# Sigmoid attention with a top-1 mixture of experts: attention in groups of two units, a joint gate for the first two batches, output stores without an order

## The chip, the cores and the metric

The kernel runs on one core of a Trainium2 chip. A core has five engines that run their own instruction queues: TensorE (PE, matrix products), VectorE (DVE), ScalarE (ACT), GpSimd (POOL) and SyncE (SP, which here only issues DMAs). They wait for one another through semaphores. The metric is the time of one launch in device microseconds, the median of three runs.

## The reference

For q, k and v of 8 batches, 12 heads, 448 tokens and 64 features in float32, attention with a sigmoid, and on its output a mixture of 8 experts that gives each token to one expert:

```python
scores = scale * np.matmul(q, k.transpose(0, 1, 3, 2)) - np.log(S)
attn = np.matmul(1 / (1 + np.exp(-scores)), v)            # 8 x 12 x 448 x 64
x = attn.transpose(0, 2, 1, 3).reshape(3584, 768)
logits = x @ w_gate                                       # 768 x 8
expert_idx = argmax(logits); gate_w = softmax(logits) at expert_idx
for e in range(8):                                        # w1: 768 x 1024, w2: 1024 x 768
    out[mask] = gate_w[mask, None] * (relu(x[mask] @ w1[e]) @ w2[e])
```

## The kernel before

**Attention** is cut into 24 units of two head pairs (a batch has three units, and `g` numbers the head pairs), and a unit into `ST` = 7 steps. `scores` (L608) makes one step's score tiles on PE, a product of 64x64 pieces into two tiles of the pool `sc` (4 buffers), and `squash` (L600) puts two sigmoids on ACT that turn them into `at` (8 buffers). `weighted` (L620) multiplies `at` by the values `vn` into two tiles `av` that gather over the 7 steps. After the seventh, `tokens` (L488) transposes the two tiles on DVE into `xt`, which SP stores to `x_tok` in DRAM once three head pairs have gathered, and `copy_tokens` (L644) copies the same tiles to `xf` on ACT, for the gate. Scores run two steps ahead of the weighted sums, so a unit starts with two steps squashed.

**The experts.** `moe` (L224) computes one slot of 448 tokens with one expert's weights, seven slots in all (`NS`). The first layer (L240) is 8 tiles of 18 matmuls of 128x128 by 448 columns, each three products of high and low parts; ACT's Relu (L247) and a DVE operation (L248) empty a tile. The second layer (L263) is 6 tiles of 24 matmuls; DVE multiplies a tile by the gate (L276) and transposes it (L277). A slot is 288 matmuls, in two alternating tiles of the pool `moe`. Weights come through SP into `wst` and are split by ACT (L159) and POOL (L160) into parts ahead of their use. `store` (L214) puts a quarter of an output tile on SP.

**The order** is written by hand: `attention` (L673) is a generator over steps `s`, 178 in all, and from step `START` = 70 on it yields twice a step, and each time 7 expert matmuls (`MIX`) are put on the queues. Steps 0 to 69 hold ten units of attention alone. From then on each unit is one burst: at its fifth step (`BURST` = 4) all its 7 steps go to PE in a row (L784 to L789), then experts again. So there are 14 bursts, and a burst can stand in the middle of an expert tile. In the burst of some units `split_tokens` (L472) prepares the next slot's tokens on DVE and ACT.

**Keys, queries and values.** `READY` (L665) loads (`load_pair`, `load_values`, 4 buffers each) and transposes (`turn`, L565, DVE) the next unit's operands at the first four steps of each unit.

**The gate** of a batch: `gate_a` (L286) makes logits of the batch's `xf` (PE, `psg`, 12 products of 32 columns), `gate_b` transposes them (PE, `pl`) and finds the best expert by small DVE operations, `gate_c` counts tokens per expert with a product by `ones` (PE, `pc`) and picks the batch's expert, `gate_d` ranks the tokens with two more products (PE, `pr`), and `gate_d2` scatters records from POOL. `PLACES` tells at which step each stage goes: those of batches 0 and 1 in the part with attention alone, at even steps, each between two pieces of attention.

## Time and profile before

| | us |
|---|---|
| median of 3 runs | 776.85 (776.73 to 777.79) |
| the profiled execution's own time | 776.84 |
| its span, first to last instruction | 775.0 |
| outside the span | 1.84 |
| attention alone, 8.6 to 125.8 | 117.2 |
| experts with 14 bursts of attention, 125.8 to 557.6 | 431.8 |
| experts alone and the end, 557.6 to 769.5 | 211.9 |

PE counts as busy 99% of the span. Its matmuls overlap in the records, since each one's end lies beyond the start of the next, so a PE that is always busy may still lose time between two kinds of work. What a matmul costs is therefore read from the distance between the starts of two rows, not from a row's length. ACT is busy 50%, DVE 48% and POOL 45% of the span.

### The profile page before, as it was taken

How to read it: one execution, taken by the hardware profiler on the slowest of the kernel's cores; microseconds unless marked ns; L12 is line 12 of the kernel's file. 1: busy time of each engine (PE TensorE's matmuls, PEld its weight loads, DVE VectorE, ACT ScalarE, POOL GpSimd, SP SyncE). 2: the span in 40 equal slices, each digit the busy share in tenths (PEclk: the TensorE clock that was granted, in tenths of full speed). 3: DMA queues.
4: the chain of work that ended last, by engine and by line, in shares of the span. 5: the costliest groups of instructions: out<-in, count | busy, mean ns of one | idle time of the engine just before them, and what ended most of it. 6: DMA issues, size and time to landing. Idle time of an engine off the chain costs nothing. (4 is left out here: it accounts for less than half of the span.)

```text
span 775.0 us, 15532 instructions
## 1 busy us (share of the span) xinstructions
PE 768.4 (99%) x5586; PEld 593.3 (77%) x5586; DVE 373.9 (48%) x806; ACT 384.1 (50%) x688; POOL 349.6 (45%) x330
## 2 busy tenths in 40 slices
PE   9999999999999999999999999999999999999997
PEld 6555557687696786867868769677698999999996
DVE  2354584465264652537426384254736493244543
ACT  5877776645536455264443653545523342444451
POOL 8648554242352342531615316054265764664351
PEclk9999999999999999999999999999999999999999
DMA  9777798976758846587585876766167554655770
GB/s 207 169 160 157 171 251 197 210 171 154 169 129 173 201 107 166 139 190 168 116 194 84 193 169 144 183 168 166 38 171 170 157 146 118 202 143 155 220 223 38
DMA packets 311633, 125.67 MB, mean 162 GB/s; under 512 B 210062, under 2 KB 307006, under 8 KB 311552
## 3 DMA queue, kind: packets, MB, share of 16 engines
q1 hardware_dynamic: 305504, 112.42, 61.9%
q0 software_dynamic: 5760, 11.76, 5.4%
q8 instruction: 45, 0.74, 0.4%
q10 hardware_dynamic: 288, 0.46, 0.2%
q14 instruction: 36, 0.29, 0.1%
HBM read 102.49 MB, written 22.49 MB: 161 GB/s over the span
## 5 line engine op out<-in xcount | busy, mean ns | idle before, releaser
L602 ACT ACTIVATE at<-sc,bias_s 128x448 f32<-128x448 f32 x336 | 192.3, 633 | 107.4 <-PE sc L616 106.5
L160 POOL TENSOR_TENSOR w1l<-wst,w1h 128x768 fp32r<-128x768 f32 x72 | 132.7, 1853 | 173.9 <-ACT w1h L159 172.2
L160 POOL TENSOR_TENSOR w2l<-wst,w2h 128x512 fp32r<-128x512 f32 x84 | 107.0, 1298 | 138.7 <-ACT w2h L159 121.0
L616 PE MATMUL sc<-qt,kt 64*64 64x448 f32 x1344 | 167.3, 545 | 0.0
L632 PE MATMUL av<-at,vn 64*64 64x448 f32 x1344 | 165.0, 536 | 0.0
L240 PE MATMUL ps<-xh,w1h 128*128 128x448 f32 x336 | 124.4, 370 | 0.2 <-DVE nw L439 0.2
L240 PE MATMUL ps<-xh,w1l 128*128 128x448 f32 x336 | 123.4, 367 | 0.0
L240 PE MATMUL ps<-xl,w1h 128*128 128x448 f32 x336 | 123.3, 367 | 0.0
L263 PE MATMUL ps<-hh,w2l 128*128 128x448 f32 x336 | 123.3, 367 | 0.0
L263 PE MATMUL ps<-hl,w2h 128*128 128x448 f32 x336 | 123.2, 367 | 0.0
L263 PE MATMUL ps<-hh,w2h 128*128 128x448 f32 x336 | 122.7, 365 | 0.0
L616 PEld LDWEIGHTS sc<-qt,kt 64*64 64x64 f32 x1344 | 78.2, 189 | 56.9 <-issue 44.4
L632 PEld LDWEIGHTS av<-at,vn 64*64 64x64 f32 x1344 | 59.4, 133 | 64.3 <-issue 53.5
L159 ACT CAST w2h<-wst 128x512 fp32r<-128x512 f32 x108 | 64.7, 620 | 75.7 <-PE ps L263 64.5
L247 ACT ACTIVATE hh<-ps 128x448 fp32r<-128x448 f32 x56 | 30.6, 546 | 139.6 <-PE ps L240 137.0
L276 DVE TENSOR_TENSOR ps<-ps,gt 128x448 f32<-128x448 f32 x42 | 40.7, 969 | 85.4 <-PE ps L263 85.3
L495 DVE STREAM_TRANSPOSE xt<-av 128x448 f32<-128x448 f32 x46 | 27.3, 629 | 101.5 <-PE av L632 100.4
L248 DVE SCALAR_TENSOR_TENSOR hl<-ps,hh 128x448 fp32r<-128x448 f32 x56 | 34.4, 614 | 78.3 <-ACT hh L247 76.8
L240 PEld LDWEIGHTS ps<-xh,w1h 128*128 128x128 f32 x336 | 63.1, 188 | 9.9 <-issue 4.4
L263 PEld LDWEIGHTS ps<-hh,w2l 128*128 128x128 f32 x336 | 65.2, 194 | 6.6 <-issue 3.5
L263 PEld LDWEIGHTS ps<-hl,w2h 128*128 128x128 f32 x336 | 65.2, 194 | 6.2 <-issue 3.2
L263 PEld LDWEIGHTS ps<-hh,w2h 128*128 128x128 f32 x336 | 65.2, 194 | 3.4 <-DVE nw L439 0.2
(158 smaller groups left out, 918.9 us busy)
## 6 DMA issues: line engine op xcount, KB each, us to landing
wst<-in_moe_w_dram SPq DMA_DIRECT2D x72, 384.0 KB, 3.3
wst<-in_moe_w_dram SPq DMA_DIRECT2D x54, 512.0 KB, 5.1
x_tok<-xt SPq DMA_DIRECT2D x64, 168.0 KB, 2.8
qn<-in_q_dram SPq DMA_DIRECT2D x184, 56.0 KB, 3.1
raw<-x_tok SPq DMA_DIRECT2D x28, 336.0 KB, 6.2
out_dram<-ob SPq DMA_DIRECT2D x84, 112.0 KB, 2.4
kn<-in_k_dram SPq DMA_DIRECT2D x104, 56.0 KB, 3.3
kn<-in_k_dram POOLq DMA_DIRECT2D x80, 56.0 KB, 4.0
```

The source lines that it names most:

```text
L159: nc.scalar.copy(hi, st)
L160: eng.tensor_tensor(lo, st, hi.bitcast(F32), op=ALU.subtract)
L240: nc.tensor.matmul(ps[:, :S], a[:, ws], b_, start=(t == 0 and n == 0), stop=(t == KD - 1 and n == 2))
L247: nc.scalar.activation(hh[:, :S], ps[:, :S], AF.Relu)
L248: nc.vector.scalar_tensor_tensor(hl[:, :S], ps[:, :S], 0.0, hh[:, :S].bitcast(F32), op0=ALU.max, op1=ALU.subtract)
L263: nc.tensor.matmul(ps[:, :S], a, b_, start=(j == 0 and n == 0), stop=(j == KF - 1 and n == 2))
L276: nc.vector.tensor_tensor(by_gate, by_gate, gate_rows[b], op=ALU.mult)
L495: nc.vector.transpose(xts[b][:, :, t, :], pv[:, :S].rearrange("p (j s) -> p j s", s=32))
L602: nc.scalar.activation(at, ps[:, :S], AF.Sigmoid, bias=bias_s, scale=SCALE)
L616: nc.tensor.matmul(ps[quarter(g, h), :S], ks, ops[g, "q"][OWN[h]], start=True, stop=True)
L632: nc.tensor.matmul(psv[g][OWN[h], :S], ops[g, "v"][rows, c, :], at[rows], start=(c == 0), stop=(c == KC - 1))
```

## The change

**Groups of two.** From step 70 on only even units have a burst, and it holds 14 steps, this unit's and the next one's: 7 groups. Within it the first two scores stand together, turns (transposes) for the unit after the next follow at steps 5, 7, 8 and 9 (`TURNS`), the first unit's tiles are emptied in the middle, and its `av` tiles are taken from the experts' pool. `to_boundary` puts the rest of the current expert tile ahead of the group, and `mixed` takes these matmuls off later yields. `gate_a` of batches 4 and 6 goes to the end of a group. The tokens of slots 1 and 3 are split in a later group (`IN_NEXT`), those of slot 5 in `moe`.

**Loads.** Pairs are loaded two units ahead and three (`FIRST_OF_TWO`), values for both units of a group while the odd unit's steps pass (`SECOND_OF_TWO`); the values of unit 11 come from POOL's queue.

**Joint gates.** Batches 0 and 1 are gated together by `early_b` to `early_d`, on tiles of both (DVE operations twice as wide), at the steps of batch 1. The ranks come from the products by `ones` and `upper` in `early_c`, so neither has a `pr`. Their eight record scatters move from steps 34 to 62 to steps 70 to 86.

**Stores.** All output stores are declared apart from one another, and `keep_tokens` puts the `x_tok` stores one yield later.

```diff
 def store():
+            nc.sync.nop()
-            apart(put, stored.setdefault((d, i), []))
+            apart(put, stored)
...
+    def early_b():
+        for b, lo in enumerate((logits_0, logits)):
+            for c in range(2):
+                at = (2 * b + c) * P
+                nc.tensor.transpose(pl[:GP, at : at + P], lo[:, c * GP : (c + 1) * GP], ident)
...
+    def early_c(oh, z):
+        for n, of in enumerate((ones, upper)):
+            nc.tensor.matmul(
+                pc[:, n * n2 : (n + 1) * n2], of[:GP], oh.rearrange("p c e -> p (c e)"), start=True, stop=True
+            )
+        nc.vector.tensor_copy(sums, pc[:, : 2 * n2])
...
+    def early_d(b, lm, sums, cnt):
+        nc.vector.tensor_copy(pre[:, 0], base)
+        for c in range(1, NCH):
+            nc.vector.tensor_add(pre[:, c], pre[:, c - 1], sums[:, 0, c - 1])
...
-                if u % 2 == 0 and s < START - ST:
+                if u % 2 == 0 and (s < START - ST or s >= START):
                     psv[g] = ps_moe.tile([P, 512], F32, tag="moe", name=f"av_{g}")
...
+    FIRST_OF_TWO = {5: lambda u: load_pair(2 * u + 6), 6: lambda u: load_pair(2 * u + 7)}
+    SECOND_OF_TWO = {i: lambda u, i=i: load_values(2 * u + 2 + i) for i in range(4)}
+    TURNS = {5: (0, "k"), 7: (0, "q"), 8: (1, "k"), 9: (1, "q")}
...
-        EARLY = {5: "b", 7: ("c", "c2"), 9: ("l", "c3"), 11: "d", 13: "g", 32: "e"}
+        EARLY = {5: "B", 7: "C", 9: ("l", "C3"), 11: "D", 13: "g", 32: "e"}
-            places = (EARLY, EARLY, FIRST_LATE, LATE, LATE, LATE, LATE, LAST)[b]
+            places = ({}, EARLY, FIRST_LATE, LATE, LATE, LATE, LATE, LAST)[b]
...
+        def to_boundary():
+            at = (NS * PER_SLOT - left) % PER_SLOT
+            one = 3 * KD if at < PER_SLOT // 2 else 3 * KF
+            return -(at - (0 if at < PER_SLOT // 2 else PER_SLOT // 2)) % one
...
-            yield s, MIX[0]
+            yield s, mixed(MIX[0])
+            keep_tokens()
             if s >= START:
+                if i == BURST and u % 2 == 0 and s < N_ST:
+                    n = to_boundary()
+                    ahead[0] += n
+                    yield s, n
...
-                if i == BURST:
-                    for n in range(ST):
-                        score_to(a + n + 3)
+                if i == BURST and u % 2 == 0:
+                    for n in range(2 * ST):
+                        score_to(a + max(n, 1) + 3)
                         weigh_to(a + n + 1)
-                        if n == ST - 1:
+                        if n == 2 * ST - 1 and u % 3 == 2:
+                            gate_a(u // 3)
+                        if n % ST == ST - 1:
                             copy_tokens()
...
+                        if n in TURNS:
+                            g, nm = TURNS[n]
+                            turn(2 * u + 4 + g, nm)
```

The next two pieces are PE's order where unit 14 (head pairs 28 and 29) ends; `sc` are scores, `av` weighted sums, `ps2` a second-layer tile. Before:

```order
L616 MATMUL sc_30_1_3705<-qt_30_3495,kt_30_3452 64x448 x2
L616 MATMUL sc_31_1_3706<-qt_31_3564,kt_31_3534 64x448 x2
L632 MATMUL av_28_3593<-at_28_6_3670,vn_28_3119 64x448 x2
L632 MATMUL av_29_3596<-at_29_6_3672,vn_29_3207 64x448 x2
L263 MATMUL ps2_1_0_0_3554<-hh_1_6_3500,w2l_1_11_3505 128x448
L263 MATMUL ps2_1_0_1_3732<-hh_1_0_3077,w2h_1_8_3413 128x448
```

The same place in the change:

```order
L742 MATMUL sc_30_1_3676<-qt_30_3466,kt_30_3423 64x448 x2
L742 MATMUL sc_31_1_3677<-qt_31_3533,kt_31_3503 64x448 x2
L758 MATMUL av_28_3572<-at_28_6_3639,vn_28_3162 64x448 x2
L758 MATMUL av_29_3575<-at_29_6_3641,vn_29_3209 64x448 x2
L742 MATMUL sc_30_2_3696<-qt_30_3466,kt_30_3423 64x448 x2
L742 MATMUL sc_31_2_3697<-qt_31_3533,kt_31_3503 64x448 x2
L758 MATMUL av_30_3706<-at_30_0_3659,vn_30_3240 64x448 x2
L758 MATMUL av_31_3709<-at_31_0_3661,vn_31_3288 64x448 x2
```

Unit 15 (head pairs 30 and 31) now follows without expert matmuls between, and the second-layer tile has been finished ahead of the group.

ACT's order at the same place; `at` are sigmoids, `xf` the copies for the gate, `w2h` weight parts. Before:

```order
L602 ACTIVATE at_30_1_3711<-sc_30_1_3705,bias_s_82 128x448
L602 ACTIVATE at_31_1_3713<-sc_31_1_3706,bias_s_82 128x448
L654 COPY xf_28_3725<-av_28_3593 128x448
L654 COPY xf_29_3727<-av_29_3596 128x448
L159 CAST w2h_1_13_3739<-wst_1_10_3182 128x512
L159 CAST w2h_1_14_3751<-wst_1_11_3376 128x512
```

In the change:

```order
L728 ACTIVATE at_30_1_3682<-sc_30_1_3676,bias_s_82 128x448
L728 ACTIVATE at_31_1_3684<-sc_31_1_3677,bias_s_82 128x448
L780 COPY xf_28_3692<-av_28_3572 128x448
L780 COPY xf_29_3694<-av_29_3575 128x448
L728 ACTIVATE at_30_2_3702<-sc_30_2_3696,bias_s_82 128x448
L728 ACTIVATE at_31_2_3704<-sc_31_2_3697,bias_s_82 128x448
```

The two copies stood behind the last sigmoid of a burst and now stand between the sigmoids of a group.

PE's order in the part with attention alone, at a gate stage; `pr` are the ranks of batch 0, `upper` and `ones` constants. Before, the stage at step 32:

```order
L632 MATMUL av_8_966<-at_8_2_931,vn_8_738 64x448 x2
L632 MATMUL av_9_969<-at_9_2_933,vn_9_798 64x448 x2
L388 LDWEIGHTS upper_90
L388 MATMUL pr_0_980<-lm_0_874,upper_90 128x32
L389 LDWEIGHTS ones_86
L389 MATMUL pr_0_980<-lm_0_874,ones_86 128x32
L616 MATMUL sc_8_4_997<-qt_8_736,kt_8_686 64x448 x2
L616 MATMUL sc_9_4_998<-qt_9_796,kt_9_740 64x448 x2
```

In the change, the joint stage at step 50:

```order
L758 MATMUL av_12_1214<-at_12_6_1289,vn_12_1041 64x448 x2
L758 MATMUL av_13_1217<-at_13_6_1291,vn_13_1087 64x448 x2
L354 LDWEIGHTS ones_86
L354 MATMUL pc_1_1328<-early_h_99,ones_86 128x64
L354 LDWEIGHTS upper_90
L354 MATMUL pc_1_1328<-early_h_99,upper_90 128x64
L742 MATMUL sc_14_1_1346<-qt_14_1158,kt_14_1146 64x448 x2
L742 MATMUL sc_15_1_1347<-qt_15_1209,kt_15_1197 64x448 x2
```

The `pr` products of batches 0 and 1 are gone; the product by `upper` stands behind the joint `pc`, with twice the columns. Batch 0's own `pl` and `pc` are gone too.

## Rows read from the trace of the kernel before

**Rows 1.** Cores: span of the core and its mean granted TensorE clock

```profile
core 0: 775.0 us, clock 1.000
```

**Rows 2.** Stages: stretch, length, busy us (x) of each engine, clock, DMA, GB/s

```profile
125.80:557.60 431.80, 431.80 (x3012) 325.62 (x3010) 211.54 (x454) 211.45 (x375) 153.47 (x113) 1.00 0.68 158
557.60:769.50 211.90, 211.71 (x1220) 197.28 (x1216) 102.39 (x189) 80.45 (x143) 111.12 (x78) 1.00 0.58 158
```

**Rows 3.** Time line of PE (start us, us, instruction): one burst

```profile
169.85 0.37 PE L263 MATMUL ps<-hh,w2h 128*128 128x448 f32 x1
170.05 0.37 PE L263 MATMUL ps<-hl,w2h 128*128 128x448 f32 x1
170.35 1.04 PE L616 MATMUL sc<-qt,kt 64*64 64x448 f32 x8
171.21 0.94 PE L632 MATMUL av<-at,vn 64*64 64x448 f32 x8
...
180.23 0.94 PE L632 MATMUL av<-at,vn 64*64 64x448 f32 x8
181.09 0.48 PE L263 MATMUL ps<-hh,w2l 128*128 128x448 f32 x1
181.41 0.37 PE L263 MATMUL ps<-hh,w2h 128*128 128x448 f32 x1
```

**Rows 4.** Time line of PE: start of the first and last burst

```profile
139.16 0.67 PE L616 MATMUL sc<-qt,kt 64*64 64x448 f32 x4
...
548.36 1.04 PE L616 MATMUL sc<-qt,kt 64*64 64x448 f32 x8
```

**Rows 5.** Time line of PE: gate matmuls of batch 0 within attention

```profile
47.97 1.70 PE L632 MATMUL av<-at,vn 64*64 64x448 f32 x16
49.61 0.43 PE L300 MATMUL pl<-ident,logits 128*112 128x128 f32 x2
49.97 1.79 PE L616 MATMUL sc<-qt,kt 64*64 64x448 f32 x16
51.58 1.70 PE L632 MATMUL av<-at,vn 64*64 64x448 f32 x16
53.22 0.19 PE L335 MATMUL pc<-oh,ones 112*128 112x32 bf16 x1
53.34 1.79 PE L616 MATMUL sc<-qt,kt 64*64 64x448 f32 x16
...
57.58 2.44 PE L632 MATMUL av<-at,vn 64*64 64x448 f32 x22
59.95 0.19 PE L388 MATMUL pr<-lm,upper 112*128 112x32 bf16 x1
...
60.09 1.40 PE L616 MATMUL sc<-qt,kt 64*64 64x448 f32 x10
```

**Rows 6.** Time line: a second-layer tile ends, DVE empties it

```profile
187.31 0.37 PE L263 MATMUL ps<-hh,w2l 128*128 128x448 f32 x1
...
187.72 0.97 DVE L276 TENSOR_TENSOR ps<-ps,gt 128x448 f32<-128x448 f32 x1 [3.23 <-PE ps L263]
...
188.72 0.65 DVE L277 STREAM_TRANSPOSE ob<-ps 128x448 f32<-128x448 f32 x1
```

**Rows 7.** Time line: end of a burst on PE, ACT, DVE

```profile
274.74 0.93 PE L632 MATMUL av<-at,vn 64*64 64x448 f32 x8
...
275.01 1.16 ACT L602 ACTIVATE at<-sc,bias_s 128x448 f32<-128x448 f32 x2 [0.33 <-PE sc L616]
...
275.70 1.18 DVE L495 STREAM_TRANSPOSE xt<-av 128x448 f32<-128x448 f32 x2 [0.80 <-PE av L632]
...
276.39 1.07 ACT L654 COPY xf<-av 128x448 f32<-128x448 f32 x2 [0.21 <-DVE xt L495]
```

**Rows 8.** Lines: a gate operation on DVE; busy us, mean ns

```profile
L322 DVE TENSOR_TENSOR oh<-eq,mr 112x32 bf16<-112x32 f32 x8 | 1.5, 191 | 0.3
```

**Rows 9.** Waits of SP: reason, us in total, times, longest us

```profile
SPq L218 <- DMA out_dram<-ob: 82.2, 50, 5.9
```

More of the change, by code (lines that the diff above doesn't have):

```diff
@@ L239, in moe @@
                 for n, (a, b_) in enumerate(((whi, xh), (whi, xl), (wlo, xh))):
-                    nc.tensor.matmul(ps[:, :S], a[:, ws], b_, start=(t == 0 and n == 0), stop=(t == KD - 1 and n == 2))
-                    yield
+                    last = t == KD - 1 and n == 2
+                    nc.tensor.matmul(ps[:, :S], a[:, ws], b_, start=(t == 0 and n == 0), stop=last)
+                    if not last:
+                        yield
                 if t == 3:
@@ L262, in moe @@
                     for n, (a, b_) in enumerate(((whi, hh), (whi, hl), (wlo, hh))):
-                        nc.tensor.matmul(
-                            ps[:, :S], a, b_, start=(j == 0 and n == 0), stop=(j == KF - 1 and n == 2)
-                        )
-                        yield
+                        last = j == KF - 1 and n == 2
+                        nc.tensor.matmul(ps[:, :S], a, b_, start=(j == 0 and n == 0), stop=last)
+                        if not last:
+                            yield
                     if (t, j) in ((0, 1), (0, 4), (0, 7), (1, 2)):
@@ L284, in tile_sigmoid_attention_top1_moe @@
     NS = B - 1
+    IN_NEXT = (1, 3)
     def gate_a(b):
@@ L294, in gate_a, with both @@
                 )
-        nc.vector.tensor_copy(logits, psg[:, :GH])
+        nc.vector.tensor_copy(logits_0 if b == 0 else logits, psg[:, :GH])
+    early = [hpool.tile([P, 2 * S], F32, tag=f"h{x}0", name=f"early_{x}") for x in "hl"]
+    logits_0 = early[1][:, :GH]
+    cuts = {}
+    def both(nm, n, words=None):
+        if nm not in cuts:
+            at = cuts.get("at", 0)
+            cuts[nm], cuts["at"] = early[0][:, at : at + (words or n)], at + (words or n)
+            assert cuts["at"] <= 2 * S
+        return cuts[nm]
@@ new lines, in early_c3 @@
+    def early_c3():
+        s1, s2 = (both_e(nm)[:GP] for nm in ("s1", "s2"))
+        nc.vector.reciprocal(s2, s2)
+        nc.vector.tensor_mul(s1, s1, s2)
+        sm = both("sm", 2 * NCH)[:GP]
+        nc.vector.tensor_reduce(sm, s1, axis=AX.X, op=ALU.add)
+        nc.vector.tensor_scalar(sm, sm, 1e-9, None, op0=ALU.add)
+        nc.vector.reciprocal(gates[:GP, :2].rearrange("p b c -> p (b c)"), sm)
+    def early_d(b, lm, sums, cnt):
+        pre, rk = (small.tile([P, NCH, E], F32, tag=nm, name=f"{nm}_{b}") for nm in ("pre", "rke"))
+        nc.vector.tensor_copy(pre[:, 0], base)
+        for c in range(1, NCH):
+            nc.vector.tensor_add(pre[:, c], pre[:, c - 1], sums[:, 0, c - 1])
+        nc.vector.tensor_add(base, base, cnt)
+        rk = rk[:GP]
+        nc.vector.tensor_add(rk, pre[:GP], sums[:GP, 1])
+        return listed(b, rk, lm)
@@ L411, in gate_d2 @@
             return
-        rec = small.tile([GP, NCH, 2], U32, tag="rec", bufs=2, name=f"rec_{b}")
+        rec = small.tile([GP, NCH, 2], U32, tag="rec", bufs=3, name=f"rec_{b}")
         nc.gpsimd.iota(
@@ L454, in tile_sigmoid_attention_top1_moe @@
     raws = {}
-    taken = [[] for _ in range(4)]
+    taken = []
     x_tok_b = x_tok.rearrange("(b j r) (i f) -> b i r j f", b=B, r=32, i=4)
@@ L708, in stage @@
             g = gate.setdefault(b, {})
-            if what == "b":
+            if what == "B":
+                g["oh"], g["z"] = early_b()
+            elif what == "C":
+                ri, *g["early"] = early_c(g["oh"], g["z"])
+                g["c"] = None, None, ri
+            elif what == "C3":
+                oh, ce, keep, cnt, sums = g["early"]
+                g["lm"] = early_c2(oh, ce, keep, cnt)
+                early_c3()
+            elif what == "D":
+                oh, ce, keep, cnt, sums = g["early"]
+                for n in range(2):
+                    si_of[n] = early_d(n, g["lm"][:, n], sums[:, :, n], cnt[:, n * E : (n + 1) * E])
+            elif what == "b":
                 g["oh"], g["z"] = gate_b(b)
@@ L754, in stages_late @@
             b, r = divmod(s - PB, PB)
-            if r == (BURST if b < B - 1 else 1) and (b + 1) * PB >= START:
+            at_end = b < B - 1 and b % 2 == 0
+            if r == (BURST if b < B - 1 else 1) and (b + 1) * PB >= START and not at_end:
                 gate_a(b)
@@ L758, in stages_late, with mixed @@
                 stage(*w)
+        ahead = [0]
+        def mixed(n):
+            less = min(n, ahead[0])
+            ahead[0] -= less
+            return n - less
+        def to_boundary():
+            at = (NS * PER_SLOT - left) % PER_SLOT
+            one = 3 * KD if at < PER_SLOT // 2 else 3 * KF
+            return -(at - (0 if at < PER_SLOT // 2 else PER_SLOT // 2)) % one
         for s in range(N_ST + 11):
```

108 lines of the change are left out of this document (94 added, 14 removed).

## Prediction

> **What bounds the kernel now.** The first view is the span and its clock: 775.0 us at a granted clock of 1.000, so there is no throttling to win or lose [rows 1]. The second is the busy time by stage: PE is busy through all 431.80 us of the stretch in which experts and attention alternate, and through 211.71 of the 211.90 us behind it, where ACT and POOL are busy half the time or less [rows 2]. PE waits for nobody; the time is the sum of what its instructions cost one after the other. The third view is therefore PE's time line, read by the distance between starts. In it the experts run at 0.20 us a matmul (169.85 to 170.05) and a set of 8 attention matmuls at 0.752 us (171.21 to 180.23 is twelve sets, 9.02 us) [rows 3]. Between the two kinds there is time that belongs to neither. A change helps here if it takes such seams or matmuls from PE, and hurts if it makes PE wait; what it moves on other engines counts only through that.
>
> **Seams of the bursts.** Going in, the first score starts 0.30 us behind the last expert matmul in place of 0.20, and the first set lasts 0.86 (170.35 to 171.21) in place of 0.75. Going out, the last set lasts 0.86 (180.23 to 181.09) and the first expert matmul 0.32 in place of 0.20 [rows 3]. That is 0.10 + 0.11 + 0.11 + 0.12 = 0.44 us a burst. Fourteen bursts, from 139.16 to 548.36 [rows 4], become seven groups: 7 x 0.44 = **3.1 us less**. The matmuls themselves stay. That a group starts at the end of an expert tile gains nothing: a tile cut in two costs its seam and no more. The gate logits that move behind a group still cost PE the same, since they stood beside a burst before.
>
> **Gate products between attention.** In the part with attention alone each gate product opens two seams too. For `pl`: the 16 matmuls ahead take 1.64 us (47.97 to 49.61) in place of 2 x 0.752 = 1.50, the products 0.36, and the 16 behind 1.61 (49.97 to 51.58): 0.14 + 0.36 + 0.11 = 0.61. For `pc`: 1.64 us ahead (51.58 to 53.22), 0.12 itself, 0.11 behind as for `pl`: 0.37. For `pr`: the 22 matmuls ahead take 2.37 us (57.58 to 59.95) in place of 22/8 x 0.752 = 2.07, the two products 0.14 (to 60.09), 0.11 behind: 0.55 [rows 5]. The change drops one `pl`, one `pc` and two `pr`: 0.61 + 0.37 + 2 x 0.55 = 2.08. The joint `pl` has two more transposes, between nothing and the 0.36 that two cost with their start; I take 0.15, since the second of a pair is pipelined behind the first. The joint `pc` has a second product, between nothing and 0.12; I take 0.05. **Net 1.9 us less**.
>
> **What the joint gate asks of DVE.** From `pl` to `pc` there are 3.25 us (49.97 to 53.22) [rows 5], into which eight small DVE operations go. One takes 191 ns on 32 columns [rows 8], so eight take 1.5 us, and even if twice the columns took twice the time they would take 3.1 us. I put no wait there. The chain behind `pc` has 14 operations in place of 8, so turns of later keys start a microsecond or two later; the scores that need them come several steps on. Nothing.
>
> **New waits at a group's start.** A group's first weighted sum writes the experts' two accumulators, one of which was filled last. After a second-layer tile DVE needs until 188.72 + 0.65 = 189.37 to empty it, 2.06 us after its last matmul began at 187.31 [rows 6]. PE is at that weighted sum 0.30 + 0.86 + 0.75 = 1.91 us after the same point, since two scores go first. That is 0.15 us short, in the two groups (units 14 and 20) that follow such a tile directly; where the logits' products stand between (units 12 and 18), or a first-layer tile ends, nothing. Two waits of 0.15: **0.3 us more** (0 to 1, if DVE has something else at hand). Behind PE's wait stand only its own matmuls.
>
> **New waits in a group's middle.** The two copies for the gate used to end a burst. Now the next sigmoids stand behind them on ACT. Take the start of the unit's last weighted sum as zero, 274.74. The copies wait for DVE's transposes and end at 276.39 + 1.07 = 277.46, that is 2.72 [rows 7]. The next pair of sigmoids, 1.16 us long (275.01) [rows 7], then ends its halves at some 3.3 and 3.9. PE makes another score at 0.75, 2.26 and 3.76, and the one at 3.76 writes the tiles that these sigmoids free. So PE waits about 0.1 us a group: **0.7 us more** in seven. The lower end is nothing. The upper end is the whole delay, 2.72 - (275.70 - 274.74) = 1.76 us a group, if ACT had no slack at all. I take 0.1, because a sigmoid pair leaves 0.33 us of ACT idle in each step [rows 7] and scores run two steps ahead.
>
> The Trainium skill, page "TensorEngine Tiling (Array Packing)", section "PSUM Bottleneck", speaks against the change here: packed small products speed up TensorE but not the emptying of PSUM, so the copies out of PSUM can become the bound. The rows show it near but not reached, 1.16 of each 1.50 us; by the rule in its strong form the sum would end on the other side, which is the third rival.
>
> **What stays free.** The independent stores lift waits off SP, which stood 82.2 us in 50 waits for earlier output stores [rows 9]; PE was waiting for none of what is queued behind them, so this gains nothing. The `x_tok` stores and up to 16 loads of pairs now gather just behind a group; queued behind them on SP are weight loads, but SP has the whole group, 21 us, to bring five raw tiles ahead. The `nop` only carries waits. POOL gets the values of unit 11 and eight scatters in the stretch where it is busy 153 of 432 us [rows 2]; behind them its weight parts wait, which later batches' scatters have done in the same place without PE waiting. The values arrive a unit sooner, never later. The splits of slots 1 and 3 move to a later group and those of slot 5 to `moe`: the same work on DVE and ACT. The longer run of experts between groups, some 196 matmuls, is no new demand: behind 557.60 PE runs 212 us of experts without bursts and waits 0.2 us [rows 2].
>
> **Sum.** -3.1 - 1.9 + 0.3 + 0.7 = -4.0, a span of 771.0 us. The profiled execution lies 776.84 - 775.0 = 1.84 us above its span, and the median of the runs is 776.85, so the same distance holds: 772.8 us.
>
> **Rivals.**
> 1. *No new wait*: the two added terms are hidden. -5.0, 771.8 us. For it: ACT's idle time in each step. Against: the 0.15 and 0.1 us are read from rows.
> 2. *DVE late in the groups that also split tokens* (units 12, 14, 18, 20). A turn stands ahead of the two transposes that the copies wait for. If these start one or two operations of some 0.6 us late (half of 1.18 us [rows 7]), PE waits 0.6 to 1.2 us in four groups: 2.4 to 4.8 us, 775.2 to 777.6. For it: DVE then has six splits in seven steps. Against: the splits end, by the same row, before 275.70, since DVE was waiting for PE there.
> 3. *ACT becomes the bound of a group*, the slower end: every group loses the full 1.76 us, 7 x 1.76 = 12.3, and with the seams and gates won the sum is -5.0 + 0.3 + 12.3 = +7.6, 784.4 us. It decides from a loss of (5.0 - 0.3 + 1.6)/7 = 0.9 us a group. For it: the copies wait for DVE, which waits for PE. Against: two steps of scores in hand.
> 4. *The change does only half of what it says*: the part with attention alone is held by ACT or DMA once the products go, and only the groups gain: -3.1 + 1.0 = -2.1, 774.7 us.
>
> **How the numbers follow.** Forecast 0.50 (772.2 to 773.6), rival 1 0.20 (771.3 to 772.2), rival 4 with its like 0.14, rival 2 0.08, rival 3 0.08. A measurement of this kernel can tell 0.2%, 1.6 us, from no change: faster is below 775.3, slower above 778.4. Faster: 0.50 + 0.20 + 0.11 = 0.81; same: 0.03 of rival 4 and 0.08 of rival 2, 0.11; slower 0.08. The range from 771.3 to 775.8 takes in the forecast, rival 1, rival 4 and the first part of rival 2, and leaves out rival 3.
>
> **What would show it.** Seven stretches of some 21.3 us of `sc` and `av` on PE in place of fourteen of 10.7; between their sets no distance above 0.9 us in the middle; `pr` six times and not eight; PE still busy 99%; and 8 matmuls of attention still at 0.752 us. The prediction is wrong if PE's waits name ACT or DVE for more than some 2 us, if `pc` waits for DVE, or if expert matmuls wait for a weight part behind a group.

## The result and the profile after

The change is **slower**: 781.88 us (median of 7, 778.68 to 786.56) against 776.85, a ratio of 1.007 [1.0055, 1.0086]. The forecast was 772.8, the range 771.3 to 775.8. All single executions of the change lie above those of the kernel before on the same chip (776.69 to 777.79).

The profiled execution took 780.08 us with a span of 778.3 (before: 776.84 and 775.0, [rows 1]). Four stretches show where the 3.3 us came in. The limits are the first attention matmul, the third batch's logits products (`psg`), the first expert matmul, the start of slot 5's second layer (slots are numbered from 0), and PE's last matmul. The columns are those of [rows 2]: stretch, length, busy us of PE, PEld, DVE, ACT and POOL, clock, DMA share, GB/s. Before:

```profile
8.61:115.71 107.10, 107.10 (x1113) 57.86 (x1109) 54.02 (x154) 82.25 (x155) 70.31 (x113) 1.00 0.85 182
115.71:125.79 10.08, 10.08 (x113) 5.23 (x113) 4.05 (x8) 7.91 (x14) 6.34 (x5) 1.00 0.87 201
125.79:610.50 484.71, 484.52 (x3288) 373.37 (x3287) 240.81 (x523) 227.97 (x404) 185.98 (x139) 1.00 0.69 159
610.50:769.40 158.90, 158.90 (x941) 149.49 (x939) 73.12 (x119) 63.94 (x114) 78.62 (x53) 1.00 0.54 155
```

After:

```profile
7.84:112.87 105.03, 105.03 (x1110) 62.81 (x1106) 48.97 (x130) 81.86 (x151) 62.60 (x104) 1.00 1.07 178
112.87:126.61 13.74, 11.50 (x115) 5.52 (x113) 8.47 (x14) 9.09 (x16) 6.50 (x6) 1.00 0.96 186
126.61:613.38 486.77, 484.93 (x3288) 397.25 (x3287) 235.94 (x521) 229.66 (x408) 196.91 (x152) 1.00 0.70 160
613.38:772.30 158.92, 158.92 (x941) 149.49 (x939) 73.17 (x120) 63.85 (x114) 77.41 (x52) 1.00 0.54 152
```

The first stretch is 2.07 us shorter, nearly as forecast. The second, the **hand-over** from attention alone to the experts, is 3.66 longer, and PE is idle for 2.2 us of it. The third was to be 2 to 3 us shorter and is 2.06 longer. (Attention also began 0.77 sooner, and behind PE's last matmul come 6.0 us in place of 5.6.) PE's waits of the changed kernel (engine, line, waited for: us, times, longest):

```profile
PE sc L742 <- DVE logits L301: 1.7, 1, 1.7
PE ps L242 <- DVE ob L281: 1.5, 1, 1.5
PE ps_warm L719 <- DVE ones L76: 1.1, 1, 1.1
PE psg L297 <- ACT xf L780: 0.6, 1, 0.6
PE ps L242 <- DVE nw L556: 0.2, 1, 0.2
```

**The hand-over**, time line of PE, DVE and POOL (start, length, instruction, then idle time before it and what ended it):

```profile
112.87 0.96 PE L297 MATMUL psg<-xf,wg 128*32 128x224 f32 x16
114.42 1.10 PE L297 MATMUL psg<-xf,wg 128*32 128x224 f32 x8 [0.58 <-ACT xf L780]
115.71 1.81 POOL L160 TENSOR_TENSOR w1l<-wst,w1h 128x768 fp32r<-128x768 f32 x1 [5.49 <-ACT w1h L159]
115.84 2.16 DVE L598 TENSOR_TENSOR xl<-whole,xh 128x448 fp32r<-128x448 f32 x1
118.48 0.34 DVE L301 COPY logits<-psg 128x224 f32<-128x224 f32 x1
118.88 0.66 PE L742 MATMUL sc<-qt,kt 64*64 64x448 f32 x2 [1.65 <-DVE logits L301]
```

From 103.8 to 118 us DVE is back to back with slot 0's six token splits and the transposes between them; the splits begin when the tokens land. PE comes 2.8 us sooner than before, DVE's splits 0.3. PE's next score shares the four `sc` buffers with `psg`, whose copy stands behind the last split on DVE.

A second thing adds to it. The last split's subtraction takes 2.16 us in place of 0.63, beside POOL's subtraction for a weight part. In the kernel before it had ended when POOL's began:

```profile
116.08 0.63 DVE L481 TENSOR_TENSOR xl<-whole,xh 128x448 fp32r<-128x448 f32 x1
116.94 1.83 POOL L160 TENSOR_TENSOR w1l<-wst,w1h 128x768 fp32r<-128x768 f32 x1 [3.83 <-ACT w1h L159]
```

The 1.53 us between them lie on the chain ahead of the logits copy and are nearly as long as PE's wait of 1.65. All eight profiles that have joint gates and slot 0's splits in their old places show 2.15 or 2.16 there; before, joint_off, and the kernels with the last two splits moved do not.

**The experts** lose at two kinds of place. One is the end of slot 1 (the expectations call it slot 2), time line of SP, DVE and PE:

```profile
293.31 2.71 SPq L625 DMA_DIRECT2D x_tok<-xt  x4
296.06 2.64 SPq L671 DMA_DIRECT2D kn<-in_k_dram  x4
...
303.62 2.88 SPq L671 DMA_DIRECT2D qn<-in_q_dram  x4
306.73 0.90 SPq L219 DMA_DIRECT2D out_dram<-ob  x2
...
310.84 0.42 SPq L219 DMA_DIRECT2D out_dram<-ob  x1
314.82 0.65 DVE L281 STREAM_TRANSPOSE ob<-ps 128x448 f32<-128x448 f32 x1 [4.63 <-DMA wst<-in_moe_w_dram]
315.62 0.44 PE L242 MATMUL ps<-xh,w1h 128*128 128x448 f32 x1 [1.54 <-DVE ob L281]
```

The slot's first output tile `ob` was complete at 296.3. Its four stores stand on SP behind the token stores and 16 pair loads that gather after a group, and go out at 306.73 to 310.84. There are two such tiles; the third needs the first one's buffer, so DVE's transpose waits 4.63 us and PE 1.54. (The trace names a weight load that landed at the same moment; in after_again the wait at this place is put down to `out_dram<-ob`.) The other place is the start of the group at unit 12, where the same wait of DVE, 1.08 us, delays the logits and the group takes 22.40 us in place of 21.43 (here and below the 1.27 us of logits products within a group are taken off).

The experts' +2.06 us are made up of some +3.4 and -1.5: slot 1's end 1.65 (the 213 matmuls between the groups at units 14 and 16 take 44.95 us, and 43.30 where nothing waits), the groups at units 12, 14 and 20 0.97, 0.18 and 0.61, against some 1.5 won at the seams.

### The profile page after: what moved, and what is told of

Read it like the earlier page. It is cut to its first block, busy times and chain, and to the rows that moved or that the text cites. A ratio compares the mean times of both kernels' runs of the same rounds, so it can differ in the third digit from the quotient of the medians.

```text
span 778.3 us, 15511 instructions
## 1 busy us (share of the span) xinstructions
PE 767.3 (99%) x5582; PEld 621.6 (80%) x5582; DVE 368.4 (47%) x785; ACT 386.5 (50%) x690; POOL 351.0 (45%) x333
## 5 line engine op out<-in xcount | busy, mean ns | idle before, releaser
L742 PE MATMUL sc<-qt,kt 64*64 64x448 f32 x1344 | 190.5, 542 | 1.8 <-DVE logits L301 1.7
L758 PE MATMUL av<-at,vn 64*64 64x448 f32 x1344 | 188.7, 537 | 0.0
L160 POOL TENSOR_TENSOR w2l<-wst,w2h 128x512 fp32r<-128x512 f32 x84 | 107.1, 1300 | 127.4 <-ACT w2h L159 121.8
L742 PEld LDWEIGHTS sc<-qt,kt 64*64 64x64 f32 x1344 | 100.3, 189 | 49.5 <-issue 29.8
L758 PEld LDWEIGHTS av<-at,vn 64*64 64x64 f32 x1344 | 77.7, 133 | 50.2 <-issue 30.0
```

The lines of the kernel that those rows point to most:

```text
L160: eng.tensor_tensor(lo, st, hi.bitcast(F32), op=ALU.subtract)
L742: nc.tensor.matmul(ps[quarter(g, h), :S], ks, ops[g, "q"][OWN[h]], start=True, stop=True)
L758: nc.tensor.matmul(psv[g][OWN[h], :S], ops[g, "v"][rows, c, :], at[rows], start=(c == 0), stop=(c == KC - 1))
```

## Experiments

Times are medians. A row is compared with runs of the kernel before on the same chip (777.3 to 777.8 in the median); the ratio and its 95% interval come from the single runs, so a ratio is not the quotient of two medians.

| run | what it is | us | ratio to before |
|---|---|---|---|
| after_again | the change, another execution | 788.1 | one run |
| joint_off | change, gates one by one | 783.5 | 1.0088 [1.0054, 1.0122] |
| first_old | change, first weight part a step sooner | 787.0 | 1.0096 [1.0059, 1.0133] |
| spread | change, pair loads parted | 784.0 | 1.0067 [1.0044, 1.0089] |
| act_stores | change, stores from ACT's queue | 782.7 | 1.0063 [1.0046, 1.0081] |
| k_pool | change, all keys from POOL's queue | 782.0 | 1.0063 [1.0046, 1.008] |
| stores_ordered | change, output stores in order again | 790.3 | 1.0163 [1.0146, 1.018] |
| hand1 | change, two splits later | 780.9 | 1.0061 [1.0031, 1.009] |
| no_stores | hand1, slots' output not stored, so its rows are missing | 776.4 | 0.9982 [0.9973, 0.9992] |
| mend1 | hand1, loads parted, stores together | 778.2 | 1.0013 [0.9997, 1.0029] |
| mend3 | mend1, loads still earlier | 777.9 | 1.0014 [0.9999, 1.0028] |
| joint_only | before, joint gates | 781.7 | 1.0055 [1.0038, 1.0072] |
| joint_hand | joint_only, two splits later | 778.4 | 1.0012 [1.0, 1.0024] |
| indep_only | before, stores independent | 776.5 | 0.9989 [0.9979, 0.9999] |
| **best1** | joint_hand, stores independent | **775.3** | **0.9969 [0.9957, 0.998]** |

### after_again: the change once more

> The changed kernel once more, to see how another execution loses its time. Theory A (the losses are at three kinds of place: the hand-over from attention alone to the experts, waits of VectorE for output stores at a group's end, and starts of the groups that split tokens): the same places show, the hand-over from the third batch's logits product to the first expert matmul takes 13 to 14 us again (10.1 in the kernel before), and what varies from execution to execution is the size of the waits for stores. Theory B (the time goes into a lower clock): the waits are as before the change, and matmuls last longer than 0.20 us in stretches away from any wait.

The hand-over took 13.44 us again. What grew is the waits for output stores: 10.2 us of DVE in two places. Time line of DVE and PE at unit 12, and the stretches from there on:

```profile
207.44 0.65 DVE L281 STREAM_TRANSPOSE ob<-ps 128x448 f32<-128x448 f32 x1 [4.19 <-DMA out_dram<-ob]
208.43 1.02 PE L742 MATMUL sc<-qt,kt 64*64 64x448 f32 x2 [3.23 <-DVE logits L301]
```

```profile
203.40:208.40 5.00, 1.79 (x16) 0.71 (x12) 0.95 (x3) 1.68 (x3) 0.00 (x0) 1.00 0.75 158
208.40:211.50 3.10, 3.07 (x20) 1.17 (x24) 3.00 (x7) 1.09 (x2) 0.00 (x0) 0.52 0.68 150
```

This group took 27.18 us, and slot 1's end lost 4.8. The theories were not alternatives: behind a wait of 3.2 us the granted clock is 0.52 for 3 us, next to the lower of its two levels (1.2 GHz, 0.5), so this wait cost half as much again. The spans of the two profiled executions differ by 7.9 us, and these two places alone by 4.8 and 3.1; the rest of the difference cancels.

### first_old: the weight part a step sooner

```diff
-    FIRST = (START - 4, START - 3, START - 1)
+    FIRST = (START - 5, START - 3, START - 1)
```

> The change with the first weight part split one step sooner, as in the kernel before. Theory A1 (the 2.16 us that one VectorE subtraction took beside POOL's subtraction of a weight part, in place of 0.62, makes the logits copy late by 1.5 us): the subtraction is back at 0.6 us and the hand-over 1.5 us shorter, 780 to 780.5. Theory A2 (VectorE's chain is late anyway): the hand-over keeps 13 us and the time 781 to 783.

Undecided: the hand-over is 13.61 us, as A2 has it, but the subtraction still takes 2.15 us, so A1's condition was never made. The weight cast waits on ACT behind the same two copies for the gate, so POOL's part falls on the same split. (The 787.0 us are above both theories: this profile has waits for output stores, 2.8 and 2.6 us of PE, as after_again has.) No run takes POOL's part away and leaves the splits in their places, so how the hand-over's loss divides between the late chain and this collision stays open.

### joint_off: batches 0 and 1 gated one by one

```diff
-        PUTS = tuple(dict(zip(range(r, r + 8, 2), FOUR)) for r in (START - PB, START + 10 - 2 * PB)) + 4 * (dict(zip((27, 28, 29, 30), FOUR)),)
+        PUTS = 2 * (dict(zip((13, 15, 17, 19), FOUR)),) + 4 * (dict(zip((27, 28, 29, 30), FOUR)),)
...
-        EARLY = {5: "B", 7: "C", 9: ("l", "C3"), 11: "D", 13: "g", 32: "e"}
-            places = ({}, EARLY, FIRST_LATE, LATE, LATE, LATE, LATE, LAST)[b]
+        EARLY = {5: "b", 7: ("c", "c2"), 9: ("l", "c3"), 11: "d", 13: "g", 32: "e"}
+            places = (EARLY, EARLY, FIRST_LATE, LATE, LATE, LATE, LATE, LAST)[b]
```

> The change without its joint gates: batches 0 and 1 are gated one by one as before, with their record scatters at the early steps. Theory A (what the joint gates save on TensorE, 1.9 us, is lost again at the hand-over, since VectorE's chain of token splits, which starts with the landing of the slot's tokens, ends no earlier): the first expert matmul starts where it did or sooner, and the time is within 1.5 us of the changed kernel's 781.9, the hand-over some 11 us. Rival (the joint gates themselves cost, or shift the record scatters into the groups, and this is the whole loss): 775 or less, with groups only gaining 3.1 us on the kernel before.

The stretch up to `psg` is 108.06 us, the hand-over 10.08, together 118.1 against 118.8 in the change: the joint gates' saving did not survive the hand-over. That is theory A, though the median, 783.5, is 1.6 us from the change's and not within 1.5; the rival's 775 is far off. The losses at output stores are there without joint gates: PE waits 1.7 us at 206 and 2.0 at 315.

### hand1: two splits behind the logits

```diff
-    SPLITS = (START - 12, START - 11, START - 10, START - 9, START - 8, START - 6)
+    SPLITS = (START - 12, START - 11, START - 10, START - 9, START - 4, START - 3)
```

> The change with the last two token splits of slot 0 moved from steps 62 and 64 to 66 and 67, behind the third batch's logits on VectorE, where it sat idle for 5 us. Theory A (VectorE's chain from the landing of slot 0's tokens is what TensorE meets at the hand-over when it comes 2.8 us sooner): the logits copy comes within 1 us of its products, the 1.7 us wait of the next score goes, the hand-over falls from 13.4 to 11 or 11.5 us, and the first expert matmul starts at 124 to 125 in place of 126.1 to 126.9: 2 us less, whatever the later waits add. Rival (ScalarE with three weight casts among its sigmoids is late anyway): hand-over still 13 us.

As theory A expects, and more. Time line of PE, no wait left:

```profile
112.99 1.34 PE L297 MATMUL psg<-xf,wg 128*32 128x224 f32 x24
114.27 1.79 PE L742 MATMUL sc<-qt,kt 64*64 64x448 f32 x16
...
123.07 0.47 PE L242 MATMUL ps<-xh,w1h 128*128 128x448 f32 x1
```

The hand-over is 10.08 us, as in the kernel before, and the first expert matmul comes 3.1 to 3.8 us sooner than in the change's other runs. The splits' move takes away both the late chain and the collision with POOL (every subtraction takes 0.62 or 0.63 us), so it does not tell them apart. Part of the gain was lost later: a new wait of 0.9 us at 135 (DVE waits 2.78 us for keys), and again slot 1's end, a wait of 2.2 us and a lower clock behind it, 3.9 us in all.

### spread, act_stores, k_pool: taking the loads from in front of the stores

spread:

```diff
-    FIRST_OF_TWO = {5: lambda u: load_pair(2 * u + 6), 6: lambda u: load_pair(2 * u + 7)}
+    FIRST_OF_TWO = {6: lambda u: load_pair(2 * u + 6)}
+    SECOND_OF_TWO[4] = lambda u: load_pair(2 * u + 5)
```

> The change with its eight pair loads behind a group moved apart: four pairs' halves at step 6, the others at step 4 of the odd unit, in place of steps 5 and 6. Theory A (output stores stand on SP behind 16 pair loads of 0.5 to 0.65 us each, the two output buffers come free late, and VectorE and then TensorE wait): the waits of VectorE for an output buffer, 5.7 us in two in the profiled execution, fall below 1 us, the group at unit 12 takes 21.6 in place of 22.4 us and the 1.9 us gap at the end of slot 2 goes: 2.5 to 4 us less, 778 to 779.5. Rival (those loads only happen to stand there; stores are late because the DMA engines are busy): the same waits elsewhere, 781 to 783.

A miss. The gap at slot 1's end went, as expected (the 213 matmuls took 43.30 us in place of 44.95). The group at unit 12 did not gain (27.86 us): the moved loads now stand ahead of it, 24 issues between 188 and 210 us, and DVE waits 5.0 us there for an output buffer. And at unit 20 the moved keys stood behind slot 4's token loads:

```profile
464.97 0.65 DVE L696 STREAM_TRANSPOSE kt<-kn 128x448 f32<-128x448 f32 x1 [8.79 <-DMA kn<-in_k_dram]
```

That group took 28.11 us, and the 784.0 us are above both theories. act_stores:

```diff
-            nc.sync.nop()
-            put = nc.sync.dma_start(
-                out_b[bass.ds(maps[n], 1)][:, :, :, cols].rearrange("o r j f -> (o r) j f"),
+            nc.scalar.nop()
+            put = nc.scalar.dma_start(
+                out_b[bass.ds(maps_a[n], 1)][:, :, :, cols].rearrange("o r j f -> (o r) j f"),
...
+    maps_a = {}
...
 def gate_e(n):
+        maps_a[n] = nc.scalar.value_load(ris[n][0:1, 1:2], min_val=0, max_val=B - 1)
```

> The change with the output stores issued from ScalarE's queue in place of SP's (ScalarE reads the batch number of a slot itself at the gate's last stage). Theory A (the stores are late because they stand on SP behind pair loads, and the two output buffers then hold up VectorE and TensorE): VectorE's waits for an output buffer, 6 to 10 us in the profiles so far, go below 1 us; the group at unit 12 takes 21.5 to 21.8 us in place of 22.4 to 27.9, the gap of 1.9 to 4.7 us behind slot 2's fourth output tile goes, no stretch of the middle shows a clock under 1; 775.5 to 778 us. Rival B (the stores are late because the DMA engines are full when a group has ended, whichever queue they come from): waits for output buffers of 4 us or more stay, 780 or more.

Half right: no wait for an output buffer is left, and the group at unit 12 takes 21.43 us. Theory A's waits are gone and rival B's are not there. The time does not follow, because now ACT's work stands behind stores that cannot go out yet. Time line of ACT:

```profile
438.32 0.32 ACTq L219 DMA_DIRECT2D out_dram<-ob  x1
438.69 0.23 ACT L448 ACTIVATE s<-z 112x32 f32<-112x32 f32 x1 [7.51 <-DMA kn<-in_k_dram]
```

The row names what the store at 438.32 waited for, the landing of a key load: the two signal the same semaphore, and the load, issued on SP at 430.17, landed at 438.30. So here a load on the other queue still holds a store up, in another way. PE waited 2.9 us there. The Trainium skill, page "Perfetto Trace Analysis", section "DMA Optimizations", says that it may make sense to give inputs one issuing engine and outputs another; here that moved the wait to the second engine, and no time was won (ratio 1.0063 against the change's 1.007). k_pool:

```diff
-                    eng = nc.gpsimd if nm == "k" and g < K_POOL else nc.sync
+                    eng = nc.gpsimd if nm == "k" else nc.sync
```

> The change with the keys of all pairs loaded from POOL's queue (before: those up to pair 21), so that half as many pair loads stand on SP ahead of the stores. Theory A: the same waits shrink by about half or go, 776 to 780 us. Rival B: no shrinking; rival C (POOL's weight parts now come late behind 13 us of issues a group): expert matmuls wait for low weight parts, above 785.

DVE's waits for buffers shrank to 1.2 us, and PE got new ones: 0.7 us for a low weight part from POOL and 1.3 us at 243, where two small DVE operations took 2.4 and 2.6 us beside POOL's work (rows of the first in the last section). The waits are theory A's, the 782.0 us are not (776 to 780), and rival C has its wait, but not its time (above 785).

### stores_ordered: the output stores in order again

```diff
-    stored = []
+    stored = {}
...
-            apart(put, stored)
+            apart(put, stored.setdefault((d, i), []))
```

> The change with the output stores of one quarter and column block in order again, as in the kernel before (each waits for the same block's store of the slot ahead). Theory A (independence alone neither cost nor gained): the same losses within their scatter, 779 to 788 us. Rival (that the stores no longer wait lets loads pile up and is what brought the losses): 775 or less.

Neither: 790.3 us. In the grouped kernel the independence of the stores is worth 7 to 8 us (by the ratios and by the medians). SP stands 79.7 us in waits for earlier stores again, and DVE waits 13.4 us in three for buffers (longest 6.9).

What the edit puts back is not quite what the expectation says. `apart(put, ...)` lifts the order between `put` and the stores in the list. Here and in the kernel before the list holds one block's stores in other slots, so these were never waited for; what is kept is the order against the other blocks. The traces show it as three stores that go out one after another's landing (first line, joint_only, a kernel with bursts and ordered stores), and without the order one behind the other (second line, best1, where the stores are apart):

```profile
475.64 6.61 SPq L218 DMA_DIRECT2D out_dram<-ob  x3
468.06 1.62 SPq L219 DMA_DIRECT2D out_dram<-ob  x3
```

### no_stores and mend1

no_stores is hand1 with the line `stores.extend(...)` taken out. mend1 is hand1 with

```diff
+    FIRST_OF_TWO = {6: lambda u: load_pair(2 * u + 6)}
+    SECOND_OF_TWO[2] = lambda u: (load_values(2 * u + 4), load_pair(2 * u + 5))
...
-                    if (t, j) in ((0, 1), (0, 4), (0, 7), (1, 2)):
-                        store()
+                    if (t, j) == (0, 2):
+                        for _ in range(4):
+                            store()
```

> hand1 (the change with slot 0's last two token splits moved) without the output stores of the seven slots: the rows of these slots are not written, nothing else is left out. An output buffer is then free as soon as its last transpose is done. Theory A: no wait for output buffers at all; what hand1 lost through them, 2.2 us in front of the first layer of slot 3, about 0.8 us in the group at unit 12 and the lower clock behind the wait, goes: 772 to 776 us. Rival (the buffers are not what PE waited for): 778 to 781, as hand1.

> The change with the split positions of hand1 (slot 0's last two token splits behind the third batch's logits), with the eight pair loads behind a group parted (four halves at step 6, the others at step 2 of the odd unit) and with all four stores of an output tile put together right behind it, at the third inner step of the next tile. Theory A (late stores behind pair loads, and VectorE's chain at the hand-over, are what cost the change its gain): hand-over 10 to 10.5 us, waits for output buffers under 2 us in all, PE's last matmul at 766 to 769 us, and 772 to 775.5 us in all, faster than both kernels. Rival (with attention's DMA traffic pressed into fewer, longer stretches, what is moved away from one place is late at another): waits for keys or weights of 3 us or more in place of those for output buffers, 778 or more.

Without stores the wait of 2.2 us at slot 1's end with the low clock behind it and the 0.8 at unit 12 are gone, and 4.5 us in the median (776.4, just above theory A's 776): output stores were hand1's largest loss. mend1 has no wait for output buffers either, and got 2.6 of these 4.5 us. Its 778.2 us miss theory A's 772 to 775.5; the rival has the time, though with a wait of 1.9 us and not 3. What both kernels still lose is mostly in the group at unit 20 (24.22 and 25.89 us in place of 21.43), again work that queues ahead of a group. Time line of ACT and PE in mend1:

```profile
458.68 0.62 ACT L159 CAST w2h<-wst 128x512 fp32r<-128x512 f32 x1 [4.97 <-DMA wst<-in_moe_w_dram]
459.89 0.70 PE L743 MATMUL sc<-qt,kt 64*64 64x448 f32 x2 [1.91 <-ACT at L729]
```

A weight cast stands ahead of the group's sigmoids on ACT, and its weights, loaded behind slot 4's tokens, land late.

### joint_only, joint_hand, indep_only, best1, mend3: one part at a time

joint_only is the kernel before with the functions `early_b` to `early_d`, their places and the later record scatters; joint_hand adds hand1's `SPLITS`; indep_only is the kernel before with a `nop` ahead of the stores and with

```diff
-            apart(put, stored.setdefault((d, i), []))
+            apart(put, stored)
...
-            taken[i].append(got)
+            taken.append(got)
...
-                for got in taken[i]:
+                for got in taken:
```

and best1 is joint_hand with the same. mend3 is mend1 with the loads at step 5 and at step 0 of the odd unit.

> The kernel before with the joint gates of batches 0 and 1 alone (their record scatters later with them): bursts of one unit, loads and stores as before. Theory A (the gates' 1.9 us are won up to the third batch's logits and given back at the hand-over, where TensorE meets VectorE's chain of token splits): from the first attention matmul to the third logits product 105 us in place of 107.1, the hand-over 13 to 13.7 in place of 10.1, the rest as before, 777 to 779 us, no better than before. Rival (the hand-over suffers from the groups' loads of values, which begin there): hand-over 10.1, 775 to 775.5.

> joint_only with slot 0's last two token splits behind the third batch's logits, as in hand1. Theory A: hand-over 10.1 us, the gates' saving arrives whole: 775.2 to 776, a bit faster than the kernel before (777.4 on these chips) and without the groups' losses. Rival (the earlier experts then meet loads that are no earlier, as hand1's wait for keys at 134 us): 776.5 to 777.5, no difference.

> The kernel before with the change's independence of stores alone (output stores apart from one another; token stores apart from all token loads). Theory A (in the kernel before the late stores are hidden: VectorE waits 4.7 us for output buffers in three places and TensorE does not): SP's 82 us of waits for earlier stores go, VectorE's waits for output buffers go or shrink, and the time stays at 776.5 to 777.5. Rival (stores that no longer wait let loads run into them): 778 or more.

> joint_hand with the independent stores, that is the kernel before with joint gates, slot 0's last two splits later and stores apart; bursts and loads as before. Theory A (what joint_hand lost, 0.65 us in the burst at 295 us and 2.7 us in the one at 485 us, it lost to output stores that wait for earlier ones on SP): these bursts are back at 10.74 us, the rest behind the first expert matmul takes 643.6 as in the kernel before, and the time is 775 to 775.8, faster than both kernels. Rival (SP's loads, not its waits, make the stores late): 777 to 778.5 as joint_hand.

> mend1 with its second half of the pair loads at step 0 of the odd unit in place of step 2 and the first at step 5 in place of 6, so that they stand well ahead of the slot's token loads. Theory A (mend1's loss of 4.4 us in the group at unit 20 comes from token loads and weight loads that land late behind these pair loads, with a ScalarE weight cast ahead of the group's sigmoids): that group back at 21.5 to 22.5 us, 773.5 to 776. Rival (the transfers there fill the DMA engines in any order): 24 us or more in that group, 777 or more.

joint_only shows the hand-over without any groups: 105.50 us to `psg`, 13.51 us of hand-over. It is worse than expected, since the bursts at 298 and 488 us also lost 0.70 and 2.22. joint_hand has a hand-over of 10.08 and the same two losses (0.65 and 2.67), so its 778.4 us are above both its theories. What the bursts wait for, time line of DVE in joint_only:

```profile
490.67 0.65 DVE L277 STREAM_TRANSPOSE ob<-ps 128x448 f32<-128x448 f32 x1 [5.60 <-DMA out_dram<-ob]
491.25 0.35 DVE L295 COPY logits<-psg 128x224 f32<-128x224 f32 x1
```

The wait is there in the kernel before too, shorter (at most 2.9 us), and TensorE does not reach it; a row of DVE's waits in the kernel before that the prediction had not read:

```profile
DVE ob L277 <- DMA out_dram<-ob: 4.7, 3, 2.9
```

indep_only removes these waits (none in its profile) and gains next to nothing, 0.9989 [0.9979, 0.9999], as the prediction said for that part. best1 removes them where they matter, and its theory A holds: all whole bursts take 10.74 us, the rest behind the first expert matmul, to the start of PE's last, 643.84 (643.58 before), and PE's waits are those of the kernel before:

```profile
PE ps_warm L706 <- DVE ones L76: 1.1, 1, 1.1
PE ps L241 <- DVE nw L551: 0.2, 1, 0.2
```

So the order of the stores is shown to cost joint_hand its two bursts. Why the waits there are longer than in the kernel before is not shown: in joint_only the experts start 1.1 us later than before, so it is not that PE comes sooner. (indep_only and best1 lift the order of the token stores against the token loads too; no run parts the two.)

best1 is faster than the kernel before by 0.3%, and so faster than the change. mend3 shows no waits for output buffers and unit 20 at 22.83 us, a little above its theory's 22.5, but PE's waits of 1.3 us at 135 (keys again), 0.9 at 444 and 0.4 at 459; its 777.9 us are the rival's. The groups, mended as far as these runs went, stay some 3 us behind the bursts of best1.

## Why the prediction was wrong

The forecast was -4.0 us; the medians moved by +5.0, and the profiled execution by +3.3. Two steps failed, both put at nothing: "What the joint gate asks of DVE" (+3.7 at the hand-over) and "What stays free" (+2.6 at output buffers in this execution, +10.5 in after_again). One of the prediction's own signs of being wrong is there: PE's waits name DVE for 1.7 and 1.5 us.

- **Early gates, -1.9**: right in size. To `psg` the change takes 105.03 us in place of 107.10, best1 105.17 (over all profiles 104.8 to 105.7 with joint gates, 107.1 to 108.1 without). The step that failed is "What the joint gate asks of DVE": turns a microsecond or two later, "nothing". It asked whether DVE delays PE behind `pc`, and not what PE, now sooner, meets next: DVE's splits, which hang on the landing of tokens and come 0.3 us sooner, and whose last one now falls on POOL's weight part (2.16 us in place of 0.62). Moving two splits (hand1, best1) brought the 1.9 back; which of the two causes weighs more is open.
- **Seams, -3.1**: mis-sized, some 1.5. An undisturbed group of 28 sets takes 21.43 us (334.35 to 355.78 below), two bursts take 2 x 10.74 [rows 3]. So a group wins 0.05 us inside, not 0.22; its seams inside are 0.37 us where a burst has 0.21. The going-out seam is the larger one: the last set lasts 1.03 us (354.75 to 355.78) in place of 0.86, and no run shows why. With the 0.22 outside, which hold, that would be 0.27 a group, 1.9 in seven. In no_stores the time from the first expert matmul to the start of PE's last is 645.82 us; less 2.79 in the group at unit 20 and 0.95 around one wait it is 642.1, against 643.58 before.

```profile
334.35 0.67 PE L742 MATMUL sc<-qt,kt 64*64 64x448 f32 x4
...
354.75 1.10 PE L758 MATMUL av<-at,vn 64*64 64x448 f32 x8
355.78 0.47 PE L242 MATMUL ps<-xh,w1h 128*128 128x448 f32 x1
```

- **Waits at a group's start, +0.3**: the mechanism holds, 21.61 us (+0.18) at unit 14 in every run with groups, but it was the small one. The large ones come from the queues.
- **Waits in a group's middle, +0.7**: none, the lower end of that term. Sets stay at 0.752 us through the middle, and the third rival falls. ACT's rows at the middle of the same group show how: six sigmoids in a row behind the copies, in time that each step otherwise leaves idle (0.34 us here).

```profile
345.88 1.06 ACT L780 COPY xf<-av 128x448 f32<-128x448 f32 x2 [0.22 <-DVE xt L612]
346.84 3.33 ACT L728 ACTIVATE at<-sc,bias_s 128x448 f32<-128x448 f32 x6
```

- **"What stays free"** is the other step that failed, and over the executions the dearer one. It asked whether PE waits for what SP holds ("PE was waiting for none of it") and gave SP the 21 us of a group for weights. It left out that output stores stand behind the same 16 loads, that there are only two output buffers, and that DVE's queue then holds logits and tile emptying behind one transpose. no_stores and mend1 show it for the groups, joint_hand and best1 for the kernel with bursts. The independence of the stores, put at nothing, is worth next to nothing in the kernel before (0.9989), 3 us behind the joint gates (joint_hand to best1) and 7 to 8 us in the groups.
- **The rivals**: the second named the right engine (DVE) and, in units 12 and 20, the right groups, with another cause: not turns in the middle, but at the start an output buffer (unit 12) and sigmoids behind a late weight cast on ACT (unit 20, shown in mend1). The third's 784.4 us lie nearest to the measured time, but that is chance: ACT bounded no group. The fourth was right that attention alone would not keep its gain, though DVE took it and not ACT or DMA, and wrong that the groups would. No case had transfers that come no sooner when PE does, so the range ended at 775.8.

## What to carry to other kernels

An engine that is busy 99% may be followed closely by a chain that nobody sees because nobody waits for it: before pricing a gain, read the waits of the engines beside it, above all those on DMAs (4.7 us on output buffers here), and ask which of them come no sooner when the bound engine does, and which operations will then run side by side that did not before. Gathering work of one kind into longer runs gathers its transfers too; what else stands on that queue, and how many buffers it has, belongs into the sum. Of a change in several parts, the part worth keeping may be a small one: joint gates, with two splits moved and stores independent, give 0.9969 without the groups.

## What the runs showed of the hardware

**A wait can cost more than its length.** In after_again two waits of PE, 3.2 us at 205 and 2.9 at 318, are each followed by about 3 us at half clock (0.52 in the row above; 0.50 from 321.2 on, where eight expert matmuls took 3.12 us in place of 1.63). Behind hand1's wait of 2.2 us at 311 the next 3 us show 0.66. Behind the waits of 1.5 and 1.65 us in the change's first profile the clock stays at 1.00. The length of a wait alone does not decide it: behind mend1's 1.9 us at 458 the next 3 us show 0.58, behind joint_off's 2.0 us at 315 they show 1.00.

**DVE operations stretch beside POOL.** A split's subtraction took 2.16 us in place of 0.62 and ended half a microsecond behind POOL's weight part (rows of the hand-over). The small gate operations, 0.19 us otherwise [rows 8], do it in the kernel before already. Time line of POOL and DVE, before:

```profile
131.09 1.84 POOL L160 TENSOR_TENSOR w1l<-wst,w1h 128x768 fp32r<-128x768 f32 x1 [5.13 <-ACT w1h L159]
131.52 1.45 DVE L317 TENSOR_TENSOR eq<-lg,mx 112x32 f32<-112x32 f32 x1
```

In k_pool, where POOL had a record scatter just ahead of each weight part:

```profile
237.70 0.99 POOL L541 DMA_INDIRECT recs<-rec,si  x1 [0.30 <-PE pl L414]
238.25 2.37 DVE L431 TENSOR_TENSOR eq<-lg,mx 112x32 f32<-112x32 f32 x1
238.72 1.85 POOL L160 TENSOR_TENSOR w1l<-wst,w1h 128x768 fp32r<-128x768 f32 x1
```

The next scatter and weight part, at 240.74 and 241.75, hold an operation of 2.55 us at 241.11 in the same way. In all three DVE's operation ends 0.04 to 0.06 us behind POOL's weight part. The Trainium skill, page "SBUF — State Buffer", section "Who interferes with whom", says that a DVE instruction with two inputs in SBUF contends with a GpSimd instruction that reads SBUF, and that issue order decides who blocks. The rows agree: POOL's record begins first, in k_pool that of the scatter (POOL's starts in a record are rough), and DVE is the one that is late. Two inputs are not needed for it: in best1 a cast with one input took 1.34 us at 119.36, in place of 0.39, beside POOL's subtraction of 118.63 to 120.45. No run took POOL's work away to test it by itself.
